# Moving a chain of small VectorE steps behind four transposes, and storing the output twice

## The chip, the cores and the metric

The kernel runs on one core of one Trainium2 chip. The time is the device time of the slowest core, here the only one, in microseconds (us). Every kernel was run several times. A text that says "median" means the median of a kernel's runs. One profiled execution of each kernel gives the lines shown below, with times counted from the start of its span.

Engines are TensorE (PE, with its weight loads as PEld), VectorE (DVE), ScalarE (ACT), GpSimd (POOL) and SyncE (SP). SyncE issues all the large loads. A load moves data from HBM, the main memory, to SBUF, the memory on the core, where one tensor named `arena` holds all buffers; 16 DMA engines do the moving, in packets. A load's "landing" is the last of its completion updates in the trace.

## The reference, cut to what matters

One token goes through two blocks, and a gate mixes the results.

```python
g = sigmoid((x * gate_w).sum(-1))
a = attention(x, k_cache, v_cache, wq, wo)   # 32 query heads, 4 key/value heads, 65536 positions, head size 128
b = mixer(B_x, w_in, w_sp, b_sp, w_out)      # gelu(x @ w_in), layer norm of one half, product of halves, @ w_out
out = g * a + (1 - g) * b                    # 1024 numbers, bfloat16
```

The two caches alone have 134 MB. With the weights, the kernel reads 162 MB. The mixer's arithmetic is tiny beside that: after its first matmul it is a chain of about twenty operations on 128 x 28 numbers or fewer.

## The kernel before

Keys and values are cut into 16 units of 4 MB each. The transposes of a key unit are done on VectorE in four pieces, and each piece feeds eight score matmuls. All large loads go through one ring of five 4 MB slots in SBUF. They are issued on SyncE in a fixed order, each as soon as the readers of its slots are done:

```python
load([("wq", 0)], ..., VB)          # query weights           8.39 MB, slots 3-4
load_k2(0, 0)                       # key units 0 and 1       8.39 MB, slots 0-1
load([("win", 0)], ..., VB)         # mixer input weights     7.34 MB, slots 3-4
load_k(2, 2)                        # key unit 2              4.19 MB, slot 2
load_k(3, 0)                        # key unit 3              4.19 MB, slot 0
load([("wout", 0)], ..., VB)        # mixer output weights    3.67 MB, slots 3-4
for i in range(6):
    a = 2 * i + 4
    if i % 3 == 2:
        load_k(a, 2)
        load_k(a + 1, 0)
    else:
        load_k2(a, (1, 0)[i % 3])   # i = 0: key units 4 and 5, slots 1-2
    load_v2(2 * i, VB)              # i = 0: value units 0 and 1, slots 3-4
...
```

So the load of key units 4 and 5 (called "the pair" below) needs slot 2, which key unit 2 occupies. It can't be issued before the last transpose of unit 2. The first value load needs slots 3 and 4, so it waits for the mixer's output matmuls, which need the result `yb` of the mixer's small steps.

The order of the work in that stage:

```python
k_step(0)
k_step(1, evac=0, own=True)
mixer_piece()            # matmuls with w_in, a copy, a transpose, then about 20 small steps ending in yb
k_step(2)                # four transposes of unit 2, 32 score matmuls
k_step(3, evac=2)
wout_piece()             # matmuls yb @ w_out
```

VectorE's timeline below shows its instructions in this order, so the small steps stand in front of the transposes of unit 2. The end of the program, cut:

```python
# for the last weights: matmuls into fb
P("DVE", lambda e: e.tensor_copy(orow[0:97, :], fb[0:97, 0:QW]), w=["orow", "fb"])
P("SP", lambda e: e.dma_start(out[0, 0].rearrange("(q n) -> q n", n=QW), osrc), r=["orow"], w=["out"], dma="out")
```

`P` records an operation with what it reads (`r`) and writes (`w`), and the semaphore waits are derived from that.

Of the kernel before, what the change touches and what calls it, by code (L numbers as in the profile page):

```python
# [131 lines left out]
def bass_gated_mix__gqa_block_cached__mixer_gmlp__decode_kernel(  # L132
# [35 lines left out]
    QW = DO // 4  # L168
# [7 lines left out]
    OFF = {}  # L176
# [15 lines left out]
    NA = (cur + 63) // 64 * 64  # L192
    arena = nc.alloc_sbuf_tensor("arena", [128, NA], BF16)

    def ab(name, n, o=0):
        return arena[:, OFF[name] + o:OFF[name] + o + n]
# [15 lines left out]
    yb, ovec, orow = ab("YB", FC), ab("OV", OC), ab("OROW", QW)  # L212
# [28 lines left out]
    P = R.op  # L241

    def mm(e, loaded, *a, **kw):

        if not loaded:
            return e.matmul(*a, **kw)  # L246
        with nc.discard():
            one = e.matmul(*a, **kw).ins  # L248
        return e.add_instruction(dataclasses.replace(one, name=nc.get_next_instruction_name(), ldweights=False))
# [8 lines left out]
                                        pattern=[[-1, 128]], channel_multiplier=1), r=["idf"], w=["idf"])  # L258
    P("POOL", lambda e: e.tensor_copy(idb, idf), r=["idf"], w=["idb"])
    P("POOL", lambda e: e.memset(qpad, 0.0), w=["qpad"])  # L260
    P("DVE", lambda e: e.memset(ones, 1.0), w=["ones"])
    P("DVE", lambda e: e.memset(oneb, 1.0), w=["oneb"])
    P("DVE", lambda e: e.memset(mb, 0.0), w=["mb"])
# [21 lines left out]
    stream = []  # L285
# [4 lines left out]
    def load(keys, src, off):  # L290

        n = len(stream)
        w = src.shape[1]
        for i, key in enumerate(keys):
            place[key] = (n, off + i * (w // len(keys)), w // len(keys))
        stream.append((keys, off, src))

    def rows(w, i, c):

        return w[128 * c * i:128 * c * (i + 1), :].rearrange("(p c) n -> p (c n)", c=c)  # L300
# [42 lines left out]
    for c0, c1 in WO_CUT:  # L343
        load([("wo", 3, c0)], rows(A_wo, 3, 8)[:, DO * c0:DO * c1], WO_AT[3] + DO * c0)

    issued = [0]
    used = set()
    owner = {}

    def grains(off, w):  # L350
        return list(range(off // GRAN, (off + w + GRAN - 1) // GRAN))

    def issue():

        while issued[0] < len(stream):
            n = issued[0]
            keys, off, src = stream[n]
            w = src.shape[1]
            gr = grains(off, w)
            if any(k not in used for x in gr if x in owner for k in owner[x]):  # L360
                return
            for x in gr:
                owner[x] = keys
            P("SP", lambda e, o=OFF["RING"] + off, w=w, src=src: e.dma_start(arena[:, o:o + w], src),  # L364
              w=[("slot", x) for x in gr], dma="s%d" % gr[0])
            issued[0] += 1

    def use(key):
        n, off, w = place[key]
        assert n < issued[0], key  # L370
        return arena[:, OFF["RING"] + off:OFF["RING"] + off + w], [("slot", x) for x in grains(off, w)]

    def done(key):
# [13 lines left out]
      r=["m32"], w=["sel"])  # L387
    P("DVE", lambda e: e.tensor_reduce(mq, vw(idf, 0, [[1, 16], [16, 8]]), AXX, ALU.add), r=["idf"], w=["mq"])
    P("DVE", lambda e: e.tensor_reduce(mhalf, vw(idf, 0, [[32, 2], [64, 2], [1, 32]]), mybir.AxisListType.XY, ALU.add),
      r=["idf"], w=["mhalf"])  # L390
# [4 lines left out]
    for fe in range(4):  # L395
        P("DVE", lambda e, fe=fe: e.tensor_copy(vw(sele, 128 * fe, [[32, 4], [1, 32]]),
                                                vw(idb, 64 * (fe // 2) + fe % 2, [[0, 4], [2, 32]])),
          r=["idb"], w=[KSE])
# [5 lines left out]
    def f(e):  # L404
# [7 lines left out]
      r=["oneb", "wsp", "bsp"], w=["mb"])  # L412
# [6 lines left out]
      r=["ones", "gs"], w=[KTB])  # L419
# [4 lines left out]
      r=["g"], w=["omg"])  # L424
# [143 lines left out]
    def mixer_piece():  # L568
        sl, keys = use(("win", 0))

        def f(e):
            for c in range(KC):
                for k in range(4):
                    for s in range(2):
                        o = F * c + FH * s + FB4 * k
                        ins = mm(e, s > 0, ob[32 * k:32 * k + 1, 512 * s:512 * s + FB4], xT[:, c:c + 1], sl[:, o:o + FB4],
                                       start=(c == 0), stop=(c == KC - 1), tile_position=(0, 32 * k),
                                       skip_group_check=True)
            return ins
        P("PE", f, r=["xT"] + keys, w=["ob"])  # L580
        done(("win", 0))
        NZ = 2 * FB4
        zr, zt = af("SC", NZ, 3 * 1024), af("SC", NZ, 4 * 1024)
        KZR, KZT = ("sc", 3), ("sc", 4)
        zw = lambda i: af("SC", 28, 3 * 1024 + 32 * i)
        zc = vw(zt, 0, [[32, 28]])
        P("DVE", lambda e: e.tensor_copy(vw(zr, 0, [[FB4, 2], [32, FC], [1, 32]]),  # L587
                                         vw(ob, 0, [[512, 2], [1, FC], [FC, 32]])), w=[KZR, "ob"])
        P("DVE", lambda e: e.transpose(zt, zr), r=[KZR], w=[KZT])  # L589
        z2, zg, ze = zw(0), zw(1), zw(2)  # L590
        P("DVE", lambda e: e.tensor_tensor(z2, zc, zc, ALU.mult), r=[KZT], w=["z2", KZR])
        P("DVE", lambda e: e.tensor_scalar(ze, z2, GELU_C, 1.0, op0=ALU.mult, op1=ALU.add), r=["z2"], w=["ze"])
        P("DVE", lambda e: e.tensor_tensor(z2, ze, zc, ALU.mult), r=["ze", KZT], w=["z2"])  # L593
        P("ACT", lambda e: e.activation(ze, z2, ACTF.Exp, scale=GELU_K), r=["z2"], w=["ze"])  # L594
        P("DVE", lambda e: e.tensor_scalar(z2, ze, 1.0, None, op0=ALU.add), r=["ze"], w=["z2"])
        P("DVE", lambda e: e.reciprocal(ze, z2), r=["z2"], w=["ze"])
        P("DVE", lambda e: e.tensor_tensor(zg, ze, zc, ALU.mult), r=["ze", KZT], w=["zg"])
        h1, h2 = zg[:, 0:FC], zg[:, FC:2 * FC]
        P("DVE", lambda e: e.tensor_reduce(col(C_T), h2, AXX, ALU.add), r=["zg"], w=["t"])
        P("PE", lambda e: e.matmul(mb[:, 0:1], ones, col(C_T), start=True, stop=True), r=["ones", "t"], w=["mb"])  # L600
        P("DVE", lambda e: e.tensor_scalar(col(C_MU), mb[:, 0:1], 1.0 / FH, None, op0=ALU.mult), w=["mu", "mb"])
        P("DVE", lambda e: e.tensor_scalar(ze[:, 0:FC], h2, col(C_MU), None, op0=ALU.subtract), r=["zg", "mu"], w=["ze"])
        P("DVE", lambda e: e.tensor_tensor(z2[:, 0:FC], ze[:, 0:FC], ze[:, 0:FC], ALU.mult), r=["ze"], w=["z2"])
        P("DVE", lambda e: e.tensor_reduce(col(C_T), z2[:, 0:FC], AXX, ALU.add), r=["z2"], w=["t"])
        P("PE", lambda e: e.matmul(mb[:, 0:1], ones, col(C_T), start=True, stop=True), r=["ones", "t"], w=["mb"])
        P("DVE", lambda e: e.tensor_scalar(col(C_V), mb[:, 0:1], 1.0 / FH, LN_EPS, op0=ALU.mult, op1=ALU.add),
          w=["v", "mb"])
        P("ACT", lambda e: e.activation(col(C_S0), col(C_V), ACTF.Sqrt), r=["v"], w=["s0"])
        P("DVE", lambda e: e.reciprocal(col(C_R0), col(C_S0)), r=["s0"], w=["r0"])
        P("DVE", lambda e: e.scalar_tensor_tensor(col(C_S1), col(C_V), col(C_R0), col(C_S0), op0=ALU.mult, op1=ALU.add),  # L610
          r=["v", "r0", "s0"], w=["s1"])
        P("DVE", lambda e: e.reciprocal(col(C_R1), col(C_S1)), r=["s1"], w=["r1"])
        P("DVE", lambda e: e.scalar_tensor_tensor(col(C_AL), col(C_R1), 2.0, wbb[:, 0:1], op0=ALU.mult, op1=ALU.mult),
          r=["r1", "wbb"], w=["al"])
        P("DVE", lambda e: e.tensor_scalar(z2[:, 0:FC], ze[:, 0:FC], col(C_AL), wbb[:, 1:2], op0=ALU.mult, op1=ALU.add),
          r=["ze", "al", "wbb"], w=["z2"])
        P("DVE", lambda e: e.scalar_tensor_tensor(yb, z2[:, 0:FC], col(C_OMG), h1, op0=ALU.mult, op1=ALU.mult),
          r=["z2", "omg", "zg"], w=["yb", KZR])
# [25 lines left out]
    def k_step(n, evac=None, gmax=None, pts=(), own=False, mid=None):  # L644

        for p in range(4):
            k_piece(n, p)
            if p == 0 and evac is not None:
                score_piece(evac)
                if gmax is not None:  # L650
                    max_first(gmax)
            if p == 1 and gmax is not None:
                max_second(gmax)
            if p == 1 and pts:
                exp_piece(pts[0])
            if p == 2 and pts:
                pt_piece(pts[0])
                exp_piece(pts[1])
            if p == 3 and pts:
                pt_piece(pts[1])  # L660
            if p == 1 and mid is not None:
                mid()
        if own:
            score_piece(n)
# [5 lines left out]

    k_step(0)
    k_step(1, evac=0, own=True)
    mixer_piece()
    k_step(2)
    k_step(3, evac=2)
    wout_piece()
    for i in range(6):
# [44 lines left out]
        P("PE", f, r=[("ovec", i)] + keys, w=["fb"])  # L722
        done(("wo", i, c0))
    P("DVE", lambda e: e.tensor_copy(orow[0:97, :], fb[0:97, 0:QW]), w=["orow", "fb"])  # L724
    osrc = bass.AP(tensor=arena, offset=OFF["OROW"], ap=[[32 * NA, 4], [1, QW]])
    P("SP", lambda e: e.dma_start(out[0, 0].rearrange("(q n) -> q n", n=QW), osrc), r=["orow"], w=["out"], dma="out")

    R.ahead = 2
    R.emit(nc)
# [28 lines left out]
```

## Time and profile before

| what | value |
|---|---|
| median of 4 runs (the rounds with the changed kernel) | 384.39 us (384.20 to 385.04) |
| span of the profiled run | 383.5 us |
| HBM read | 162.01 MB |
| share of the load queue's packets, 16 engines | 98.2% |
| VectorE, TensorE busy | 55%, 59% |

The profile page cuts the span in 40 slices. The first row is the busy share of the DMA engines in tenths, the second what they moved; the third line is from the queue table (packets, MB, share):

```profile
DMA  9999999989999999989999999999999999999995
GB/s 438 431 437 431 396 415 431 429 368 437 426 437 431 431 426 424 437 383 431 444 439 437 437 437 431 431 439 425 437 410 422 468 437 437 437 400 436 408 423 236
...
q1 hardware_dynamic: 4184, 162.01, 98.2%
```

Most slices move 431 to 437 GB/s. The ninth, from 77 to 86 us, has 368. The load stream is the bound, and this is a place where it was not full.

The windows view shows the same stretch more closely (columns as in its head line; the last two are the DMA share and GB/s):

```profile
core 0: us, PE busy (x) PEld busy (x) DVE busy (x) ACT busy (x) POOL busy (x), PEclk, DMA share, GB/s
77.00:87.00 10.00, 8.62 (x28) 1.69 (x15) 8.27 (x5) 0.00 (x0) 0.00 (x0) 0.71 0.77 333
87.50:90.00 2.50, 2.22 (x11) 0.38 (x4) 2.50 (x4) 0.00 (x0) 0.00 (x0) 1.00 0.30 105
90.00:107.00 17.00, 8.56 (x62) 1.64 (x34) 6.82 (x7) 2.31 (x2) 0.00 (x0) 0.89 1.00 433
```

From 77 to 87 us the queue moved 333 GB/s, about 100 less than a full stretch. Over 10 us that is 1 MB, or 2.3 us of the full rate: this is the hole. Shorter windows need care, because the view counts a packet whole where it starts, and a load packet of 64 KB takes 2.4 us. Asked for 85 to 87.2 us, the view gives 39 GB/s and a DMA share of 0.10. The packet records agree: the engines ran out of work one after another from 85.1 us on, and the pair's first packets started at 87.22.

VectorE's timeline says what came before it (start, duration, engine, line, operation; in brackets the idle time before it and what ended that):

```profile
68.35 1.11 DVE L589 STREAM_TRANSPOSE arena<-arena 128x896 f32<-128x896 f32 x1
69.50 0.20 DVE L591 TENSOR_TENSOR arena<-arena 128x28 f32<-128x28 f32 x1
...
75.23 0.23 DVE L617 SCALAR_TENSOR_TENSOR arena<-arena 128x14 bf16<-128x14 f32 x1
75.38 4.50 DVE L475 STREAM_TRANSPOSE arena<-arena 128x2048 f32<-128x2048 f32 x2
81.38 2.31 DVE L475 STREAM_TRANSPOSE arena<-arena 128x2048 f32<-128x2048 f32 x1 [1.50 <-PE scp L248]
83.92 4.51 DVE L475 STREAM_TRANSPOSE arena<-arena 128x2048 f32<-128x2048 f32 x2 [0.23 <-PE scp L248]
```

The small steps run from 69.50 to 75.46, 6.0 us. Unit 2's transposes come only after them, and the fourth of the five transposes that start at 75.38 to 83.92 ends unit 2 at 86.26. The chain of waits follows that directly into the pair's load (start, duration, what):

```profile
83.92 2.32 DVE arena L475
86.26 22.91 DMA arena<-in_A_k_cache_dram
109.19 2.32 DVE arena L475
```

SyncE's issues show how late this was:

```profile
67.22 0.33 SPq L364 DMA_DIRECT2D arena<-in_B_w_out_dram  x1
86.26 0.33 SPq L364 DMA_DIRECT2D arena<-in_A_k_cache_dram  x1
99.98 0.33 SPq L364 DMA_DIRECT2D arena<-in_A_v_cache_dram  x1
```

The mixer's output weights were issued at 67.22 and landed at 87.61. The pair was issued at 86.26, only 1.35 us ahead of that landing. It landed at 109.17, 21.56 us after it. Most other 8.39 MB loads, which were queued in good time, landed 19.35 us after the load before them. The difference, 2.2 us, is the hole.

The end of the program:

```profile
381.37 0.42 DVE L724 CAST arena<-fbt 97x256 bf16<-97x256 f32 x1 [9.98 <-PE fbt L718]
381.82 0.63 SPq L726 DMA_DIRECT2D out_dram<-arena  x1
```

The last weights landed at 380.89. Four matmuls, the cast, the store's issue (0.63 us) and its landing made up the 2.6 us to the end of the span.

### The profile page before, as it was taken

To read this page: it belongs to the slowest core of one execution; us is meant where nothing else is said; L and a number is where in the kernel's file an instruction comes from. 1 tells how busy PE (TensorE), PEld (TensorE's weight loads), DVE (VectorE), ACT (ScalarE), POOL (GpSimd) and SP (SyncE) were. 2 spreads that over 40 slices of the span, in tenths; PEclk is the share of its full clock that TensorE was granted. 3 is DMA by queue.
4 is the path that set the end of the run, shared out by engine and by line. 5 is a ranking of instruction groups with operands and counts; after the bars stand their busy time and mean duration, and the time that the engine had idled before them with its cause. 6 is when DMAs were issued, how large, how long until landed. Compare 5 with 4: busy or idle time off the path is not lost.

```text
span 383.5 us, 2499 instructions
## 1 busy us (share of the span) xinstructions
PE 224.8 (59%) x1375; PEld 55.5 (14%) x785; DVE 210.7 (55%) x229; ACT 25.3 (7%) x39; POOL 1.5 (0%) x8
## 2 busy tenths in 40 slices
PE   0061479187437863687855728781779643859373
PEld 0010012111011210121211101120212100212031
DVE  4112596789069805984992049934993990242020
ACT  1000000100203000100210001000200100121000
POOL 1000000000000000000000000000000000000000
PEclk9996599669858995999698968995899996969776
DMA  9999999989999999989999999999999999999995
GB/s 438 431 437 431 396 415 431 429 368 437 426 437 431 431 426 424 437 383 431 444 439 437 437 437 431 431 439 425 437 410 422 468 437 437 437 400 436 408 423 236
DMA packets 4230, 162.16 MB, mean 423 GB/s; under 512 B 504, under 2 KB 508, under 8 KB 764
## 3 DMA queue, kind: packets, MB, share of 16 engines
q1 hardware_dynamic: 4184, 162.01, 98.2%
q8 instruction: 8, 0.13, 0.1%
q14 instruction: 2, 0.02, 0.0%
q10 hardware_dynamic: 36, 0.00, 0.0%
HBM read 162.01 MB, written 0.00 MB: 422 GB/s over the span
## 4 chain that ended last, share of the span: by engine, by line
DMA 57%; DVE 24%; PE 18%; issue 1%; SPq 0%; ACT 0%; DVEq 0%
DMA arena<-in_A_k_cache_dram 39%; DVE arena L475 18%; DMA arena<-in_A_v_cache_dram 10%; DMA arena<-in_A_wo_dram 8%; PE scp L246 6%; PE scp L248 5%; PE obt L246 3%; PE obt L248 3%; DVE arena L513 2%; DVE arena L492 1%; PE fbt L718 1%; DVE arena L589 0%; DVE arena L587 0%; PE mbt L500 0%; SPq L364 0%
## 5 line engine op out<-in xcount | busy, mean ns | idle before, releaser
L475 DVE STREAM_TRANSPOSE arena<-arena 128x2048 f32<-128x2048 f32 x64 | 145.0, 2289 | 73.0 <-DMA arena<-in_A_k_cache_dram 62.3
L246 PE MATMUL scp<-arena 128*128 128x512 bf16 x256 | 106.7, 417 | 94.1 <-DVE arena L475 91.2
L248 PE MATMUL scp<-arena 128*128 128x512 bf16 x256 | 106.1, 414 | 0.0
L246 PE MATMUL obt<-arena 128*64 128x512 bf16 (+2 forms) x334 | 63.1, 421 | 22.1 <-DMA arena<-in_A_v_cache_dram 22.1
L248 PE MATMUL obt<-arena 128*64 128x512 bf16 (+2 forms) x334 | 62.4, 417 | 0.0
L246 PEld LDWEIGHTS scp<-arena 128*128 128x128 bf16 x256 | 26.5, 104 | 195.9 <-DVE arena L475 121.0
L508 ACT ACTIVATE arena<-arena 128x1024 bf16<-128x1024 f32 x16 | 18.4, 1148 | 227.8 <-DVE arena L513 115.9
L246 PEld LDWEIGHTS obt<-arena 128*64 128x64 bf16 (+1 forms) x334 | 18.3, 113 | 76.9 <-issue 59.0
L492 DVE TENSOR_SCALAR_CACHE_REDUCE arena<-scp 128x1024 f32<-128x1024 f32 x16 | 19.0, 1190 | 16.7 <-PE scp L248 16.7
L513 DVE STREAM_TRANSPOSE arena<-arena 128x1024 bf16<-128x1024 bf16 x16 | 19.4, 1213 | 8.9 <-PE obt L248 6.4
L538 DVE RECIPROCAL arena<-mbt 128x1 f32<-128x1 f32 x4 | 0.7, 168 | 26.3 <-PE mbt L534 26.3
L718 PE MATMUL fbt<-arena 128*1 128x256 bf16 x128 | 6.7, 376 | 4.0 <-DMA arena<-in_A_wo_dram 4.0
L406 PE MATMUL scp<-arena 8*128 8x1 bf16 x8 | 0.7, 200 | 10.9 <-DVE arena L401 10.9
L411 PE MATMUL mbt<-arena 1*128 1x2 bf16 x1 | 0.2, 159 | 10.2 <-DMA arena<-in_B_b_sp_dram 10.2
L724 DVE CAST arena<-fbt 97x256 bf16<-97x256 f32 x1 | 0.4, 425 | 10.0 <-PE fbt L718 10.0
L413 DVE COPY arena<-mbt 128x2 f32<-128x2 f32 x1 | 0.2, 158 | 10.2 <-PE mbt L411 10.2
L553 PE MATMUL mbt<-arena 128*128 128x128 bf16 x16 | 2.0, 262 | 4.7 <-DVE arena L548 4.7
L718 PEld LDWEIGHTS fbt<-arena 128*1 128x1 bf16 x128 | 3.4, 105 | 7.2 <-DMA arena<-in_A_wo_dram 3.6
L440 DVE CAST arena<-obt 97x1024 bf16<-97x1024 f32 x1 | 1.2, 1224 | 5.3 <-PE obt L248 5.3
L463 DVE COPY arena<-arena 32x32 bf16<-32x32 bf16 x16 | 2.6, 165 | 2.2 <-PE scp L248 2.0
L559 DVE TENSOR_TENSOR arena<-mbt,arena 128x128 f32<-128x128 f32 x4 | 1.2, 291 | 4.4 <-PE mbt L553 4.4
L594 ACT ACTIVATE arena<-arena 128x28 f32<-128x28 f32 x1 | 0.2, 226 | 46.7 <-DVE arena L593 46.7
(88 smaller groups left out, 52.3 us busy)
## 6 DMA issues: line engine op xcount, KB each, us to landing
arena<-in_A_k_cache_dram SPq DMA_DIRECT2D x6, 4096.0 KB, 33.4
arena<-in_A_v_cache_dram SPq DMA_DIRECT2D x2, 4096.0 KB, 24.2
arena<-in_B_w_in_dram SPq DMA_DIRECT2D x1, 7168.0 KB, 30.4
arena<-in_A_wo_dram SPq DMA_DIRECT2D x3, 2048.0 KB, 29.0
arena<-in_B_w_out_dram SPq DMA_DIRECT2D x1, 3584.0 KB, 20.4
arena<-in_A_wo_dram SPq DMA_DIRECT2D x1, 1280.0 KB, 31.3
arena<-in_A_wo_dram SPq DMA_DIRECT2D x1, 512.0 KB, 32.0
arena<-in_A_wo_dram SPq DMA_DIRECT2D x1, 256.0 KB, 32.1
```

Source lines behind the costliest of these rows:

```text
L246: return e.matmul(*a, **kw)
L248: one = e.matmul(*a, **kw).ins
L406: ins = e.matmul(tb[:, c:c + 1], vw(xm, c, [[8, 128]], 0, 8), oneb[0:8, 0:1], start=(c == 0), stop=(c == KC - 1), skip_group_check=True)
L440: P("DVE", lambda e: e.tensor_copy(psb[0:97, :], ob[0:97, :]), w=["psb", "ob"])
L463: P("DVE", lambda e, pb=pb: e.tensor_copy(vw(qpad, 24 + 32 * pb, [[QP, 4], [1, 8]], 32 * pb, 32), vw(qall, 8 * g, [[32, 4], [1, 8]], 32 * ...
L475: P("DVE", lambda e: e.transpose(ktb(i).bitcast(F32), sl[:, 4096 * p:4096 * (p + 1)].bitcast(F32)), r=keys[4 * p:4 * p + 4], w=[("kt", i % ...
L492: P("DVE", lambda e: e.tensor_scalar(scs(n), sc_ps(n), 0.0, None, op0=ALU.add, op1=ALU.max, accum_out=maxc[:, n:n + 1]), w=[("sc", n % NSC ...
L508: P("ACT", lambda e: e.activation(psb, scs(n), ACTF.Exp, bias=gcol(n // NP, K_NB), scale=SCALE, accum_out=lp[:, n:n + 1]), r=[("sc", n % N ...
L513: P("DVE", lambda e: e.transpose(ptsb(n), psb), r=["psb"], w=[("ptsb", n % 2)])
L553: ins = e.matmul(mb[:, 0:128], sel[:, 128 * c:128 * (c + 1)], osc[:, 128 * c:128 * (c + 1)], start=(c == 0), stop=(c == 3))
L559: P("DVE", lambda e: e.tensor_tensor(vw(ot, 0, [[8, 16], [1, 8]]), vw(mb, 0, [[8, 16], [1, 8]]), vw(mq, 0, [[1, 16], [0, 8]]), ALU.mult), ...
L718: ins = e.matmul(fb[32 * q:32 * q + 1, 0:QW], ovec[:, 8 * i + c:8 * i + c + 1], sl[:, o:o + QW], start=False, stop=(i == 3 and c == 7), ti ...
```

## The change

The intent has two parts. First, the small steps go behind unit 2's transposes, so that slot 2 comes free earlier. Second, the output is stored once with zeros while the last weights load, so that the store at the end is not the first of its kind.

```diff
+    P("POOL", lambda e: e.memset(orow, 0.0), w=["orow"])
...
+    def store():
+        P("SP", lambda e: e.dma_start(out[0, 0].rearrange("(q n) -> q n", n=QW), osrc), r=["orow"],
+          w=["out"], dma="out")
...  in issue():
+            if n == len(stream) - 1:
+                store()
...  in mixer_piece(), after the copy and the transpose:
+        return zw, zc, KZR, KZT
+
+    def mixer_rest(zw, zc, KZR, KZT):
         z2, zg, ze = zw(0), zw(1), zw(2)
...
-    mixer_piece()
+    mix = mixer_piece()
     k_step(2)
+    mixer_rest(*mix)
     k_step(3, evac=2)
...
-    P("SP", lambda e: e.dma_start(...), r=["orow"], w=["out"], dma="out")
+    store()
```

More of the change, by code (lines that the diff above doesn't have):

```diff
@@ L344, in bass_gated_mix__gqa_block_cached__mixer_gmlp__decode_kernel @@
         load([("wo", 3, c0)], rows(A_wo, 3, 8)[:, DO * c0:DO * c1], WO_AT[3] + DO * c0)
+    osrc = bass.AP(tensor=arena, offset=OFF["OROW"], ap=[[32 * NA, 4], [1, QW]])
+    def store():
+        P("SP", lambda e: e.dma_start(out[0, 0].rearrange("(q n) -> q n", n=QW), osrc), r=["orow"],
+          w=["out"], dma="out")
     issued = [0]
@@ L724, in bass_gated_mix__gqa_block_cached__mixer_gmlp__decode_kernel @@
     P("DVE", lambda e: e.tensor_copy(orow[0:97, :], fb[0:97, 0:QW]), w=["orow", "fb"])
-    osrc = bass.AP(tensor=arena, offset=OFF["OROW"], ap=[[32 * NA, 4], [1, QW]])
-    P("SP", lambda e: e.dma_start(out[0, 0].rearrange("(q n) -> q n", n=QW), osrc), r=["orow"], w=["out"], dma="out")
+    store()
     R.ahead = 2
```

## The prediction

> **What bounds the kernel now.** The load queue. The slice table gives DMA 90% or more in nearly every slice, the queue table 98.2% of the span, 162.0 MB read; a full slice moves 431 to 437 GB/s. VectorE is busy 55%, TensorE 59%. Time can only come from holes in the load stream and from the two ends.
>
> **The hole.** The slice from 77 to 86 us has 368 GB/s, and fine windows show almost nothing moved from 88.5 to 90. The mixer's output weights were issued at 67.2 and landed 20.4 us later, at 87.6 (DMA issues). The next load, the key pair 4/5 (8.39 MB), needs unit 2's slot and was issued only when that unit's fourth transpose ended, at 86.26; it landed at 109.17 (chain of waits). From 87.6 that is 21.6 us; at 434 to 437 GB/s it takes 19.2 to 19.4. So the hole is about 2.2 us: the issue came 1.35 us ahead of the previous landing, too late to cover its own start-up. After 109 I find no second hole of this kind: later loads are issued 7 us or more before the previous lands, until the last at 348.7.
>
> **First part of the change.** In the VectorE timeline unit 2's transposes start at 75.38, behind the mixer's small steps (69.50 to 75.46, 6.0 us, mostly 0.2 us operations with TensorE and ScalarE round trips). Unit 2 had landed at about 69.5. Now its transposes start there. Four took 10.9 us before, because the TensorE clock was halved and VectorE waited for a transposed buffer; so they end, and the load is issued, at about 80 (78.5 to 80.5), 7 us before the weights land. The hole closes: -2.2 us. No work is removed; the small steps move to about 80 to 86, and their statistics matmuls now queue behind unit 2's last score matmuls (0 to 1.7 us of extra wait). Unit 3 then starts near 86, as before, possibly on a halved clock: the Trainium skill, "TensorE: Matmul & The Clock Gate", Part 1, says about 3.4 us of idleness halves it; this trace's 0.50 at 70 to 82 agrees. The mixer's output matmuls may thus end 0 to 2.5 us later than 100. The next value load needs that, but has until about 103 before a new hole opens (key pair landing at 107).
>
> **Second part.** The last landing is at 380.9; then four matmuls, a 0.42 us cast, and a store whose issue takes 0.63 us on SyncE against 0.33 for other issues after a wait. The ACT queue's first small load took 0.58, the next three 0.27 to 0.28. I read that as a first-use cost; a zero store before it should save about 0.3 us at the very end. Its own costs: one 0.1 us-class memset on an idle POOL, 2 KB in the queue, and perhaps up to 0.3 us if the final weights' completion waits for the store's write on four engines ("DMA: Bandwidth & Descriptors", HWDGE ordering). Net -0.2.
>
> **Time.** 384.44 - 2.2 - 0.2 = 382.0 us; 381.3 to 383.2 should hold 8 in 10. Faster by over 2%: 0.01; within: 0.98; slower: 0.01.
>
> **What would show it.** The key pair issued near 80 and landing near 107; no slice of 368 GB/s there; every later landing 2.2 us earlier; last weights at about 378.7; second store's issue near 0.33 us.
>
> **What would make it wrong.** The mixer's output matmuls past 103, opening a hole before the value load; the queue's rate limited elsewhere so the hole returns; the zero store delaying the last load or the cast that overwrites its source; no first-use cost.

## The result, and the profile after

The changed kernel took 382.62 us, the median of 4 runs (382.36 to 382.84), against 384.39 before. The ratio of the two is 0.9951 with a 95% interval of 0.9933 to 0.9968. Ratios here are the mean time of one kernel's runs over that of the other's runs of the same rounds, so not quite the ratio of the quoted medians. The span of the profiled run is 381.5 us. The gain of about 1.8 us is clear of noise.

The page's slices and queue after (the same rows as before):

```profile
DMA  9999999999999999999999999999989999999995
GB/s 440 433 426 405 440 386 436 437 485 443 428 433 405 405 435 440 440 419 436 443 428 440 440 440 440 435 440 434 440 378 414 460 440 433 433 411 429 417 424 212
...
q1 hardware_dynamic: 4192, 162.01, 98.6%
```

The ninth slice no longer stands out below the rest. The windows (same columns):

```profile
77.00:87.00 10.00, 4.50 (x20) 1.36 (x12) 8.04 (x21) 1.71 (x3) 0.00 (x0) 0.90 1.01 434
87.50:90.00 2.50, 2.50 (x7) 0.44 (x3) 2.50 (x3) 0.00 (x0) 0.00 (x0) 0.50 0.97 419
```

From 77 to 87 us the queue now moved 434 GB/s instead of 333. From 85 to 87.2 us no engine ran out of work any more: the view gives 503 GB/s instead of 39 (over 440 because it counts packets by their start). VectorE's timeline:

```profile
69.39 4.51 DVE L484 STREAM_TRANSPOSE arena<-arena 128x2048 f32<-128x2048 f32 x2 [0.26 <-DMA arena<-in_A_k_cache_dram]
75.16 4.51 DVE L484 STREAM_TRANSPOSE arena<-arena 128x2048 f32<-128x2048 f32 x2 [1.27 <-PE scp L248]
79.59 0.17 DVE L603 TENSOR_TENSOR arena<-arena 128x28 f32<-128x28 f32 x1
...
84.89 0.23 DVE L629 SCALAR_TENSOR_TENSOR arena<-arena 128x14 bf16<-128x14 f32 x1
85.04 2.31 DVE L484 STREAM_TRANSPOSE arena<-arena 128x2048 f32<-128x2048 f32 x1
```

Unit 2's transposes start at 69.39, as soon as the unit has landed, and the small steps come from 79.59 on. Unit 3 starts at 85.04. The chain of waits and the issues:

```profile
75.16 4.51 DVE arena L484 x2
...
79.69 27.24 DMA arena<-in_A_k_cache_dram
...
106.96 2.31 DVE arena L484
```

```profile
66.89 0.33 SPq L373 DMA_DIRECT2D arena<-in_B_w_out_dram  x1
79.69 0.33 SPq L373 DMA_DIRECT2D arena<-in_A_k_cache_dram  x1
99.38 0.33 SPq L373 DMA_DIRECT2D arena<-in_A_v_cache_dram  x1
```

The pair was issued at 79.69, 7.9 us ahead of the landing of the mixer's output weights (87.57), and landed at 106.93. That is 19.36 us after that landing, like any load that is queued in time. Against 109.17 before, it is 2.24 us earlier. The value load was issued at 99.38, no later than before.

The end:

```profile
379.45 0.42 DVE L737 CAST arena<-fbt 97x256 bf16<-97x256 f32 x1 [9.72 <-PE fbt L731]
379.91 0.54 SPq L350 DMA_DIRECT2D out_dram<-arena  x1
```

The store's issue takes 0.54 us instead of 0.63.

### The profile page after: what moved, and what is told of

Its sections match the earlier page's. It is cut to its first block, busy times and chain, and to the rows that moved or that the text cites. A ratio compares the mean times of both kernels' runs of the same rounds, so it can differ in the third digit from the quotient of the medians. Undisturbed runs are those within 1.5% of the kernel's fastest.

```text
span 381.5 us, 2501 instructions
## 1 busy us (share of the span) xinstructions
PE 223.8 (59%) x1375; PEld 54.6 (14%) x785; DVE 210.4 (55%) x229; ACT 25.4 (7%) x39; POOL 1.8 (0%) x9
## 4 chain that ended last, share of the span: by engine, by line
DMA 63%; DVE 21%; PE 13%; SPq 1%; issue 0%; ACTq 0%; DVEq 0%
DMA arena<-in_A_k_cache_dram 40%; DVE arena L484 16%; DMA arena<-in_A_v_cache_dram 10%; DMA arena<-in_A_wo_dram 8%; DMA arena<-in_B_b_sp_dram 5%; PE obt L246 3%; PE obt L248 3%; PE scp L246 3%; PE scp L248 3%; DVE arena L522 2%; DVE arena L501 1%; SPq L373 0%; ACTq L272 0%; SPq L350 0%; PE scp L427 0%
## 5 line engine op out<-in xcount | busy, mean ns | idle before, releaser
L246 PE MATMUL obt<-arena 128*64 128x512 bf16 (+2 forms) x334 | 63.8, 423 | 22.0 <-DMA arena<-in_A_v_cache_dram 22.0
L248 PE MATMUL obt<-arena 128*64 128x512 bf16 (+2 forms) x334 | 63.1, 418 | 0.0
```

What stands on the lines that cost most here:

```text
L246: return e.matmul(*a, **kw)
L248: one = e.matmul(*a, **kw).ins
```

## The experiments

All kernels gave correct results. Medians are of 4 to 6 runs, each beside runs of the kernel before on the same chip in the same rounds. There were three sets of rounds:

| run | median us | before, same rounds | ratio | 95% interval |
|---|---|---|---|---|
| e1_mixer_only | 382.49 | 384.72 | 0.9948 | 0.9934 to 0.9963 |
| e2_store_only | 384.41 | 384.72 | 1.0005 | 0.9986 to 1.0024 |
| e3_split_load | 382.60 | 384.72 | 0.9951 | 0.9937 to 0.9965 |
| e4_half_front | 382.75 | 384.72 | 0.9956 | 0.9941 to 0.9971 |
| e5_slack3 | 384.16 | 384.42 | 0.9981 | 0.9957 to 1.0005 |
| e6_slack8 | 388.83 | 384.42 | 1.0110 | 1.0097 to 1.0124 |
| e7_store_early | 382.62 | 384.42 | 0.9949 | 0.9937 to 0.9960 |
| e8_both (the change, again) | 382.58 | 384.42 | 0.9948 | 0.9936 to 0.9960 |
| e9_issue_85 | 384.71 | 384.96 | 0.9991 | 0.9975 to 1.0007 |
| e10_issue_88 | 387.41 | 384.96 | 1.0061 | 1.0044 to 1.0079 |
| e11_act_store | 382.58 | 384.96 | 0.9938 | 0.9923 to 0.9953 |
| e12_mixer_again | 382.57 | 384.96 | 0.9939 | 0.9924 to 0.9955 |

The theory is that the gain is one hole in the load queue, closed by an earlier issue. The main rival is that the gain comes from the better order on VectorE and TensorE as such.

### Each part alone

e1 is the changed kernel without the zero store, e2 is the changed kernel with the small steps back in front:

```diff
# e1
-    P("POOL", lambda e: e.memset(orow, 0.0), w=["orow"])
-            if n == len(stream) - 1:
-                store()
# e2
-    mix = mixer_piece()
-    k_step(2)
-    mixer_rest(*mix)
+    mixer_rest(*mixer_piece())
+    k_step(2)
```

> The mixer's order of the change, without the zero store. Theory (the load queue had one hole of about 2.2 us before the loads of key units 4 and 5): nearly the whole gain is here, 1.7 to 2.3 us under the kernel before; pair issued near 80, landing near 107. The store's issue at the end takes about 0.63 us again. Rival (the store gives a good part of the gain): this run gains less than 1.5 us.

> The zero store of the change, with the mixer's steps where they were. Theory: the hole stays (pair landing near 109.2) and the time is that of the kernel before within 0.3 us; the final store, issue to last landing, is about 0.06 us shorter than before's 1.64, as in the changed kernel's trace. My prediction said 0.2 to 0.3 us. Rival: 0.5 us or more either way, faster by a warmed path or slower by a late completion of the last weights.

e1 gained 2.2 us on its median, e2 0.3 us, which its interval (0.9986 to 1.0024) can't tell from nothing. In e1 the pair landed at 106.66, in e2 at 108.56. The whole gain that can be measured is the mixer's order. The control e8, which has both parts, is at 382.58; e1 on its own set of rounds is at 382.49, and repeated as e12 at 382.57.

### The hole closed without touching the order

```diff
# e3, on the kernel before
+        elif i == 0:
+            load_k(a, 1)
+            load_k(a + 1, 2)
         else:
             load_k2(a, (1, 0)[i % 3])
```

> The kernel before, with key units 4 and 5 as two loads of 4 MB instead of one of 8: unit 4's slot has been free since about 62, so its load no longer waits for unit 2's transposes. The order on VectorE is untouched. Theory (hole in the load queue): the hole closes as well, unit 5 lands near 107, 1.7 to 2.3 us under before. Rival (the gain comes of VectorE reaching unit 2 earlier, or of fewer waits between VectorE and TensorE): within 0.4 us of before.

Here VectorE does the small steps first, as before. Only unit 4's half of the pair no longer waits for slot 2. SyncE's issues in e3:

```profile
67.40 0.33 SPq L367 DMA_DIRECT2D arena<-in_B_w_out_dram  x1
67.77 19.09 SPq L367 DMA_DIRECT2D arena<-in_A_k_cache_dram  x2
100.25 0.33 SPq L367 DMA_DIRECT2D arena<-in_A_v_cache_dram  x1
```

Unit 4's load went out right behind the mixer's output weights. (The second line merges it with unit 5's, which was issued at 86.53, as late as in the kernel before.) By then 4 MB were still queued, so the lateness cost nothing: unit 5 landed at 107.03. The time is that of the change, 382.60 us. So the earlier transposes are not needed for the gain, only a queue that stays full.

### The new order kept, the hole put back

These two hold back only the pair's issue, in the changed kernel. `late` names what the issue has to wait for.

```diff
# e9: late = ["yb"], the mixer's last small step;  e10: late = [("sc", 2)], the maxima of unit 2
             n = issued[0]
+            if n == 6 and not late:
+                return
...
             P("SP", lambda e, ...: e.dma_start(arena[:, o:o + w], src),
-              w=[("slot", x) for x in gr], dma="s%d" % gr[0])
+              r=late if n == 6 else [], w=[("slot", x) for x in gr], dma="s%d" % gr[0])
```

> The changed kernel, with only the load of key units 4 and 5 held back until the mixer's last small step, so it is issued near 85 instead of 79.5; VectorE and TensorE keep the new order. Theory: the hole is back in part, 3.6 us less the lead over the mixer weights' landing (87.3 - 85 = 2.3), so about 1.3 us (0.8 to 1.8) slower than the changed kernel. Rival (the new order itself gives the gain): as fast as the changed kernel.

> As e9, held back until the maxima of unit 2 are taken, near 88.4. Theory: hole 3.6 + 1.1 = 4.7 us (4.0 to 5.4), slower than the changed kernel by that and so 2 to 3 us slower than the kernel before, although its VectorE order is the new one. Rival: as fast as the changed kernel.

The pair's load in the chain of waits of e9:

```profile
85.03 23.15 DMA arena<-in_A_k_cache_dram
```

And of e10:

```profile
88.73 23.16 DMA arena<-in_A_k_cache_dram
```

e9 landed the pair at 108.19, and e10 at 111.89. The new order on VectorE was in place in both, and yet e9 is 2.1 us and e10 4.8 us slower than e12 of the same rounds (384.71 and 387.41 against 382.57; e12 has no zero store, which by e2 makes no measurable difference). e10 is as expected, and it is 2.45 us slower than the kernel before. e9's median is a little over the expected 0.8 to 1.8. Its profiled run was its fastest (383.60), and in that trace the pair lost 1.4 us. The other five runs, 384.51 to 384.91, left no trace, so where they lost about 1 us more is open. The rival falls with this pair of runs: the order as such gave nothing that shows.

### Half of the small steps in front

```diff
# e4: mixer_rest cut behind the mean's subtraction
-    mix = mixer_piece()
+    mix = mixer_rest(*mixer_piece())
     k_step(2)
-    mixer_rest(*mix)
+    mixer_last(*mix)
```

> The changed kernel, but with the mixer's steps up to the mean's subtraction (3.0 of 6.0 us) again ahead of unit 2's transposes. Theory: the pair is issued near 83, still ahead of the last moment that covers its start-up (estimate 84: the weights' landing at 87.6 less the 3.6 us by which the issue in before was late, 1.35 + 2.2), so the time is that of the changed kernel within 0.4 us. Rival (each us moved from in front of unit 2 saves its share): about 0.9 us slower than the changed kernel.

The pair was issued at 82.39, 2.7 us later than in the change, and the median is 0.26 us above e1's of the same rounds. A share of half the gain would have been about 1 us. So most of the gain is there as soon as the lead is long enough, and issuing still earlier adds little. The profiled run was e4's slowest (383.36; the other five are between 382.38 and 382.79), and its trace lost a further 0.9 us near 292 us, at a place that the edit doesn't touch.

### How much room the mixer's output matmuls have

e5 and e6 put dummy memsets behind the small steps, and so delay unit 3, the mixer's output matmuls and the value load's issue:

```diff
     mixer_rest(*mix)
+    for _ in range(3):        # e6: 8
+        P("DVE", lambda e: e.memset(ob, 0.0), r=["lull"], w=["lull", "ob"])
```

> The changed kernel with three memsets of the free accumulator (0.9 us each) behind the mixer's small steps, so unit 3, the mixer's output matmuls and the issue of the first value load come about 2.9 us later (near 102). Theory: the load of values 0 and 1 is still in time (last moment about 103.3: the pair's landing at 106.9 less 3.6), so no change within 0.4 us. Rival (VectorE's chain bounds this stage): about 2.9 us slower.

> As e5 with eight memsets, about 7.6 us later: the value load is issued near 107, after the pair's landing. Theory: a new hole of issue time less 103.3, that is 3 to 4 us, and all of it in the total, since every later load is queued back to back. If the total rises by 7 us, VectorE's chain bounds; if by less than 1 us, later slack takes the hole up.

Each memset took 1.2 us with its wait, not the 0.95 that I had counted, so the value loads were issued later than planned: at 103.13 in e5, and in e6 as here:

```profile
109.39 0.33 SPq L373 DMA_DIRECT2D arena<-in_A_v_cache_dram  x1
```

e6 lost 5.4 us at the landing of that value load and 1.1 at the next, and its total is 6.25 us above e8's. My number was 3 to 4 us, for an issue at 107. With the issue measured, 109.39 less the last moment of 103.3 gives 6.1, close to what was lost. Nothing took the hole up later, and the delay on VectorE (10.0 us at the issue) didn't go into the total either.

e5 is a miss, and inconclusive as a bound. Its issue stood 3.7 us ahead of the pair's landing (106.81), just at the edge, and the value load lost 0.8 us. A further 1.4 us was lost near 351 us, at a place that the edit doesn't touch. Two of its six runs were at 382.6, as fast as the change; the others were between 383.97 and 385.19.

### The holes in one table

The lead is the landing of the load before, less the issue. The interval is from that landing to this load's own. The excess is the interval less 19.35 us. All are from the profiled runs' issue and landing records, one trace each. The rows with a lead over 6 us are a selection.

| kernel | load | lead us | interval us | excess us |
|---|---|---|---|---|
| changed kernel | pair | 7.9 | 19.36 | 0.0 |
| e8 | pair | 7.8 | 19.46 | 0.1 |
| e12 | pair | 7.7 | 19.35 | 0.0 |
| before | key units 6, 7 | 7.2 | 19.55 | 0.2 |
| e5 | pair | 7.1 | 19.36 | 0.0 |
| e4 | values 0, 1 | 6.7 | 19.35 | 0.0 |
| e4 | pair | 4.8 | 19.82 | 0.5 |
| e5 | values 0, 1 | 3.7 | 20.12 | 0.8 |
| e9 | pair | 2.4 | 20.74 | 1.4 |
| e2 | pair | 1.6 | 21.30 | 1.9 |
| before | pair | 1.35 | 21.56 | 2.2 |
| e10 | pair | -1.2 | 24.40 | 5.0 |
| e6 | values 0, 1 | -2.7 | 24.73 | 5.4 |

From a lead of 2.4 us downwards the excess is about 3.6 to 3.8 us less the lead, except for e6, whose next load brings the missing 1.1. From 6.7 us upwards it is mostly nothing, with single losses, most of 0.1 to 0.5 us, that do not follow the lead (0.2 at 7.2 us in the kernel before, but 0.0 at 7.1 in e5 and 6.7 in e4). Between the two, the traces lost 0.8 us at 3.7 and 0.5 at 4.8. With one trace each, and e4's and e5's medians so different (0.3 and 1.6 us above e1 and e8), how soft the edge is there is not shown.

### The store

e7 issues the zero store ahead of the fourth load, at about 29 us, instead of among the last weights. e11 is e1 with the only store issued from ScalarE's queue:

```diff
# e7
-            if n == len(stream) - 1:
+            if n == 3:
# e11, on e1
-        P("SP", lambda e: e.dma_start(out[0, 0]...
+        P("ACT", lambda e: e.dma_start(out[0, 0]...
```

> The changed kernel with the zero store issued ahead of the fourth load, at about 29 us, instead of ahead of the last weights. Theory (a small first-use cost): the final store is as in the changed kernel, issue about 0.54 us, issue to landing about 1.58 us; the time is the same within 0.3 us. Rival (the zero store among the last weights holds their completion up): 0.3 us or more faster. Rival (what is warm cools within 30 us): the final issue takes the same in both, so the gap from 0.54 to 0.33 is not age.

> The changed kernel unaltered, as the control of this chip and these rounds: 1.5 to 2.2 us under before.

> The mixer's new order, no zero store, and the only store issued from ScalarE's queue, which has issued four small loads at the start (0.58 us the first, 0.27 to 0.28 the next). If the store's issue time is first use of a queue by small transfers, it is 0.3 us here and the time 0.2 to 0.3 us under the run of the mixer's order alone. If it belongs to a store, or to its four-partition shape, it is 0.5 to 0.65 us and the time is the same within 0.2 us.

> The mixer's new order alone, as the control of this chip and these rounds: 1.7 to 2.3 us under before.

The final store's issue took 0.54 us in the traces of all kernels with a zero store, and 0.62 or 0.63 in those without one that store from SyncE (before, e1, e3, e12). In e7 the zero store is about 350 us old instead of 33, and the issue takes the same, so age plays no part. In e11 it took 0.58:

```profile
379.60 0.58 ACTq L349 DMA_DIRECT2D out_dram<-arena  x1
```

ScalarE's queue had issued four small loads at the start, the last three in 0.27 to 0.29 us. Taken alone, e11 leaves a rival: the queue had issued nothing for 377 us, and its first load took 0.57 us too, so it may have gone cold again. The zero stores settle it for SyncE: the changed kernel's, at 347.10, was issued 0.05 us behind the issue of a load on the same queue, e7's, at 28.75, likewise, and both took 0.63 us. So most of the 0.6 us belongs to a store of this form, not to first use of the queue; what part of the form (direction, four partitions of 512 bytes) makes it costly stays open. e11 is as fast as e12.

The 0.09 us that the zero store saves did not reach the end. From the start of the store's issue to its landing it is 1.59 us in the changed kernel and 1.64 before, so only 0.06 of it is left there. The chain of waits at the end of e12, without a zero store:

```profile
378.42 0.41 PE fbt L728 x4
378.83 0.02 issue
378.86 0.42 DVE arena L734
```

And of the changed kernel:

```profile
378.95 0.41 PE fbt L731 x4
379.36 0.03 issue
379.39 0.02 DVEq L109
379.41 0.04 issue
379.45 0.42 DVE arena L737
```

In the changed kernel a second wait (DVEq L109, the recorder's line for waits) stands between the last matmul and the cast. The zero store reads `orow`, so the cast, which writes `orow`, must wait for it too. The wait was satisfied long before, but passing it costs: from the matmuls' end to the cast it is 0.09 us (379.36 to 379.45) against 0.03 (378.83 to 378.86). That pays back the 0.06. The traces agree on it: from the end of the last matmul's record to the cast it is 0.12 us in all nine traces with a zero store and 0.05 in the five without. From the last weights' landing to the store's own it is 2.58 us before, 2.57 in e1 and e12, and 2.59 in the changed kernel.

## Why the prediction was right or wrong

**The bound and the hole: right.** The load queue bounds the kernel, and its one hole of this size lay ahead of the pair. e3 closed it with the old order and gained the same. e9 and e10 opened it again with the new order and lost the gain.

**Its size, 2.2 us: right at the place, smaller at the end.** The pair landed 2.24 us earlier. The last weights landed 1.98 us earlier (378.91 against 380.89). The medians differ by 1.8 us, and in the other sets of rounds e8 gained 1.8, e1 2.2 and e12 2.4; the kernel before varies by itself from 383.7 to 385.6 over all rounds, while e1, e3, e7, e8, e11 and e12 stay between 382.28 and 382.78. Why the kernel with the hole scatters more is open. In the traces, the landings' gain first grew from 2.24 to 2.5 us by 264 us, mostly because the kernel before lost 0.2 us more at key units 6 and 7. Then 0.5 us of it was given back at one place: the value load landing near 281.5 took 19.84 us after the load before it in the changed kernel, but 19.35 in the kernel before and 19.34 in e9. It took 19.74 to 19.86 in e1, e7 and e8, and 19.54 in e12. Each trace shows a packet of 8 KB of the queue kind "instruction" between 260 and 273 us, and behind it one load packet of about 3 us where others take 2.42 (3.08 in the changed kernel, 2.95 before). The Trainium skill, "DMA: Bandwidth & Descriptors", section "Queues, rings and completion order", lists runtime-internal traffic as queue row 14, on the same engines as the loads, and the trace agrees: the packet is on queue 14, in the midst of the load stream (at 265.7 us in the changed kernel). If the packet meets an engine that is already the last, the landing moves; the engines' first and last completion updates of one load are 1.98 us apart before that place and 2.47 after it. That it meets the slowest engine in some kernels and not in others was not tested, and the trace doesn't name the engine. Each trace also has eight "instruction" packets of 16 KB on queue 8 after 50 us, and most of them cost no landing anything. This cause is argued, not shown.

**The issue near 80: right** (79.69). As I wrote, TensorE's halved clock made VectorE wait for a transposed buffer: 1.27 us in the changed kernel, 1.50 and 0.23 before. The extra wait of 0 to 1.7 us that I allowed the small steps did not come: they took 5.5 us (79.59 to 85.12) against 6.0.

**The room for the mixer's output matmuls: right that there is some.** I had allowed 0 to 2.5 us of delay; there was none, 99.38 against 99.98, because unit 3 started at 85.04 instead of 86.2. The halved clock for unit 3 that I mentioned did come (0.50 from 87.5 to 90 us in the windows view), as the Trainium skill, "TensorE: Matmul & The Clock Gate", Part 1, has it after idle windows of about 3.4 us, and the value load was still issued no later. The trace agrees if the small steps' two pairs of one-column matmuls (81.55 and 82.86) are left out: the clock record has the half from 85.0 us, 3.4 us after the last full matmul ended (81.64) but only 1.8 us after the last of those. Which of the two counts, no run here shows. The last moment of 103 that I gave is the edge that e5 sat on and e6 overstepped.

**The store, -0.2 us: wrong in its size.** The step that failed was: "I read that as a first-use cost; a zero store before it should save about 0.3 us at the very end." The issue fell by 0.09 us, not 0.3, because the comparison with ScalarE's small loads didn't carry over to a store: the zero store took 0.63 us right behind a load on SyncE's queue, and e11's store 0.58 on ScalarE's. And the cast's second wait cost 0.06 us, a term that I had named only as a risk. At the end nothing is left (2.58 and 2.59 us above), and e2 measured no gain. The harm that I feared, late completion of the last weights, was not seen either: e7 and e8, with the zero store early and late, differ by 0.04 us.

**The time:** predicted 382.0 us, measured 382.62, inside the range. Predicted was a gain of 2.4 us, and the medians show 1.8. Of the 0.6 us between them the store explains 0.2. The rest is of the size of what the load stream gave back after the pair's landing, and of the scatter of the kernel before.

No experiment gave a version that beats the changed kernel: e1, e3, e7, e11 and e12 are all within 0.15 us of it. The simplest that is as fast is e1, the mixer's order without the second store.

## What to carry to other kernels

In a kernel whose load queue is full, ask of each issue not whether it comes before the queue runs dry, but by how much: here an issue with 6.7 us or more of lead over the landing before it was free, but for single losses that did not follow the lead, two single traces with 4.8 and 3.7 lost 0.5 and 0.8 us, and below 2.4 us every further us of lead lacking was lost and did not come back. What frees the slot should run first on its engine, and small steps that nothing large waits for can go behind it; splitting a load so that half of it depends on less does the same without moving any work. A store in advance to "warm" the path brought nothing, and the wait that it added on the buffer took back what it saved. And where a view counts packets by their start, a window as short as a packet can show a hole where there is none: here the landings, and a window of 10 us, gave the size.

## What the Trainium skill lacked or had wrong

- "DMA: Bandwidth & Descriptors", Specifications, gives 0.6 us to the first byte for loads issued from SyncE. The trace is near it (first packets of the pair 0.96 us after the start of an issue that takes 0.33, so 0.63 after its end). What the page lacks is what a late issue costs a running stream: 2.2 us at a lead of 1.35 us, and 5.0 us at a lead of -1.2. An estimate from numbers for the kernel before: 2.0 us because the engines finish the load ahead at different times (first to last completion update), 0.96 us to the first packets, and 0.65 us because the first packets after the hole took about 3.1 us instead of 2.42, in sum 3.6.
- The same page says, in section "iDMA fabric" and within an explanation that it calls unconfirmed, that a bulk load runs at the pace of its slowest engine, but no page that I read says how far the 16 engines drift apart within one stream of loads: 0.6 us between the first and last completion update of a load at 41 us, 2.0 at 60 us, 2.4 at the end of the changed kernel.
- No page that I read tells a store's issue time from a load's: 0.62 us for a small store from SyncE, 0.58 from ScalarE, 0.54 for a second one, against 0.33 for a large load issued after a wait and 0.43 for one issued right behind another.
- No page that I read has the cost of one more semaphore wait that is already satisfied: 0.06 us ahead of the cast.
